# Attention and gated experts on one core: the order of the early expert tiles' transposes, gathers and activations

## The chip, the cores and the metric

One core of a Trainium2 chip runs the whole program. The metric is the device time of one execution in microseconds, from launch to end. Before the change the median of 3 runs is 470.3 us (469.93 to 471.26).

## What is computed

The inputs are q, k and v of shape (4, 8, 768, 64), a decay per head, a gate matrix of 8 experts with one more column for "local", and the experts' weights w1 (8, 512, 1024) and w2 (8, 1024, 512), all in fp32. First comes linear attention with decay, block by block along the sequence; its output is laid out as x with 3072 tokens of 512 numbers. Then each token goes through one expert:

```python
fresh_e = int(np.argmax(logits[b, s]))
e = fresh_e if s == 0 or local_gate[b, s] < 0.5 else prev_e
p = softmax(logits[b, s])
h = np.maximum(x[b, s] @ w1[e], 0.0)
out[b, s] = p[e] * (h @ w2[e])
```

The expert of a token can so depend on the token before it.

## The kernel before, in words

**Attention, 24 steps.** A step handles 128 tokens of one batch. TensorE makes scores, products with the state and the transposed output (lines 186 to 281); ScalarE copies the rows of x to `xn`, and a DMA writes them to `x_dram` (`rows_of`, line 269). `gates` and `logits` (lines 283 to 297) make the gate's logits of four steps at a time. Routing is computed on the side: `fresh_experts`, `along_sequences`, `experts_of`, `chances`, `ranks`, `masks` (lines 383 to 482), in three parts of the tokens, the third (i = 2) after the last step. `brought` and `by_slots` (lines 590 to 631) turn tokens into slots: `brought` is VectorE work, `by_slots` a sum on TensorE over all tokens that gives the token index of each slot (`gidx`), and its gate.

**The early tiles.** The routing of the first half of the tokens is known early, so five tiles of 128 tokens of one expert each (tiles 0 to 4) are computed while the second half is still being routed. A tile is: gather 128 rows of x (`ahead`, an indirect DMA issued by GpSimd, into `xgt[0]` or `xgt[1]` in turn); turn them so that the features lie on partitions (`xtt`); `hidden` for each half of the 1024 hidden numbers (64 TensorE instructions in all, then a Relu on ScalarE, line 738); `output` (16 TensorE instructions, line 742); `written` (gate on VectorE, line 768, and a scatter). Turning without TensorE takes two steps: `flipped` (line 716), one VectorE transpose of 32x32 blocks into `xqs[0]` (the tile `xlast`) or `xqs[1]` (the tile `lg`), and `moved` (line 720), 16 ScalarE copies of 32 partitions x 128 elements (line 725) that put the blocks in their places. `turned_in_blocks` is both. `turned` (line 710) does it with four TensorE transposes and a copy out of PSUM.

**The later tiles.** Tokens that remain go in pairs of tiles of one expert (`pair`, line 974), computed as a Winograd product of 7 instead of 8 block products: `sums_1`, `sums_2` and `sums_of_x` (lines 936 to 948) are VectorE sums of weight blocks and of x, `product_1` (line 953) and `product_2` (line 958) are TensorE. Within a pair numbered hooks take the steps of half tiles (`hooks_of_halves`, line 1123) and of others. With this data there are also three full tiles between pair 2 and pair 3 (`full`, line 1216).

**What sets the order.** Inside `manual_schedule` each named engine runs its instructions in the order in which the code writes them. For the attention and the early tiles these are TensorE, VectorE, SyncE and GpSimd, and ScalarE's order comes from a scheduler; from line 1175 on they are TensorE, VectorE, SyncE and ScalarE. Weights come over SyncE's queue (`weights`, line 670, skipped if the buffer already holds the expert; `weights_of`, line 677) into two buffers of w1 and w2 each, and a third that is shared by half and full tiles and, before that, by the 0/1 array that `brought` writes. From the early tiles to the first pair the code before reads, with the lines of the change in it:

```python
        turned_in_blocks(1)            # 902: tile 3, behind tokens_to_other_tiles
        hiddens(2); finished(2); weights(4)
        brought(1, (0, 1, 2, 3, 4))    # 906
        turned_in_blocks(0)            # 907: tile 4
        hiddens(3)                     # 908
        by_slots(1, (0, 1, 2, 3, 4))   # 910
        finished(3)                    # 912
...
        hidden(0, 0, 0)                # 1182: tile 4
        hidden(0, 0, 1)
        pair_turned(0); sums_1(0, range(4)); output(0, 0); pair_turned(1)
        sums_of_x(0)                   # 1188, then pair 0
```

Of the kernel before, what the change touches and what calls it, by code (L numbers as in the profile page):

```python
# [8 lines left out]
F32 = mybir.dt.float32  # L9
# [55 lines left out]
def kernel(  # L65
# [203 lines left out]
    def rows_of(s):  # L269
        px = pg.tile([P, DM], F32, name="pk1")  # L270
        for a in range(A):
            nc.tensor.transpose(px[:, P * a:P * a + P], xc[:, a, ORDER[s][0]], ident)
        if s + 1 < NS:
            xn = att.tile([P, DM], F32, name="xn", bufs=4)
        else:
            xn = xlast
        nc.scalar.copy(xn, px)


        queue = nc.scalar if s + 3 < NS else nc.sync  # L280
        queue.dma_start(out=x_dram[P * s:P * s + P, :], in_=xn)

    def gates(k):

        for d in range(DT):
            nc.tensor.matmul(pl[EP * d:EP * d + EP], lhsT=wgt[:, d], rhs=xc[:, d].rearrange("p b i -> p (b i)"),
                             start=True, stop=True, skip_group_check=True)
        lg = lgs[k] = rt.tile([P, B * P], F32, name="lg")
        nc.scalar.copy(lg, pl)
# [86 lines left out]
    def pool(i):  # L376
        return pools[i == 2]
# [5 lines left out]
    def fresh_experts(i):  # L383

        lo, hi = PARTS[i]
        n = hi - lo
        lg = lt[:, lo:hi, :E]
        if not i:
            nc.vector.memset(lt[0:1, :B, E:], -1.0)
        mx = nows["mx", i] = pool(i).tile([P, n], F32, name=f"mx{i}", bufs=1)  # L390
        nc.vector.tensor_reduce(mx, lg, axis=AX.X, op=ALU.max)
        top = pool(i).tile([P, n, E], F32, name=f"top{i}", bufs=1)
        nc.vector.tensor_tensor(top, lg, mx.unsqueeze(2).broadcast_to([P, n, E]), ALU.is_equal)
        nc.vector.tensor_tensor(top, top, down.unsqueeze(1).broadcast_to([P, n, E]), ALU.mult)
        best = pool(i).tile([P, n], F32, name=f"best{i}", bufs=1)
        nc.vector.tensor_reduce(best, top, axis=AX.X, op=ALU.max)
        mark = nows["mark"] = pool(i).tile([P, n], BF16, name=f"mark{i}", bufs=1)
        nc.vector.scalar_tensor_tensor(mark, lt[:, lo:hi, E], FRESH, best, ALU.is_le, ALU.mult)

    def along_sequences(i):  # L400
# [269 lines left out]
    def weights(g):  # L670

        experts[g] = e = expert(g)
        other = e != experts[g - 2]
        nc.sync.dma_start(out=w1t[g % 2], in_=w1_src(e), cond=other, cond_hint=False)
        nc.sync.dma_start(out=w2t[g % 2], in_=w2_src(e), cond=other, cond_hint=False)
# [8 lines left out]
    def w_of(p):  # L684
        return (p + 1) % 2
# [16 lines left out]
    def ahead(g, i):  # L702
        collect(xgt[i], *at(g))
# [3 lines left out]
            nc.tensor.transpose(pr[:, P * d:P * d + P], xgt[0][:, P * d:P * d + P], ident)  # L707
        nc.vector.tensor_copy(xtt[0].rearrange("p d i -> p (d i)"), pr)

    def turned(i, xt=None, copy=nc.vector.tensor_copy, xg=None):  # L710
        pt = pg.tile([P, DT, P], F32, name="po1")
        for d in range(DT):
            nc.tensor.transpose(pt[:, d], (xgt[i] if xg is None else xg)[:, P * d:P * d + P], ident)
        copy(xtt[i] if xt is None else xt, pt)

    def flipped(xq, xg):

        nc.vector.transpose(xq, xg)  # L718

    def moved(xt, xq, ks=range(4)):  # L720

        blocks = xq.rearrange("p (d j i) -> p d j i", j=4, i=QP)
        for k in ks:
            for j in range(4):
                nc.scalar.copy(xt[QP * j:QP * j + QP, :, QP * k:QP * k + QP], blocks[QP * k:QP * k + QP, :, j])  # L725

    def turned_in_blocks(i, xg=None):
        flipped(xqs[i], xgt[i] if xg is None else xg)
        moved(xtt[i], xqs[i])

    def hidden(i, w, half):
        ph = pg.tile([P, FT // 2, P], F32, name=f"ps{half}")
        for j in range(FT // 2):
            f = FT // 2 * half + j
            for d in range(DT):
                nc.tensor.matmul(ph[:, j], lhsT=w1t[w][:, d, P * f:P * f + P], rhs=xtt[i][:, d],  # L736
                                 start=(d == 0), stop=(d == DT - 1))
        nc.scalar.activation(hq[half, i], ph, ACT.Relu)  # L738

    def output(i, w):  # L740
        for f in range(FT):
            nc.tensor.matmul(pys[i], lhsT=hq[f // 4, i][:, f % 4], rhs=w2t[w][:, f], start=(f == 0), stop=(f == FT - 1))  # L742

    def apart(rows):
# [45 lines left out]
    with tc.manual_schedule(engines={PE, DVE, SP, POOL}):  # L790
# [16 lines left out]
        for s in range(NS):  # L807
            if s + LOADS - 1 < NS:
                loaded(s + LOADS - 1)
            if s + 3 < NS and s != 1:  # L810
                prepare(s + 3)
            if s in QUARTERS:
                j = QUARTERS.index(s)
                nc.sync.dma_start(out=w1t[0][:, j], in_=w1_src(0)[:, j])
            if s == NS - 4:
                nc.sync.dma_start(out=w2t[0], in_=w2_src(0))
                weights(0)
            if s == NS - 1:
                nc.sync.dma_start(out=w1t[1], in_=w1_src(1))
                nc.sync.dma_start(out=w2t[1], in_=w2_src(1))  # L820
                weights(1)
            if s + 1 < NS and s not in (1, 2, 3, 4, 5):
                scores(s + 1)
            from_state(s)
            if s % B == 1 and s > B:
                logits(s // B - 1)
            if s == 5:
                scores(6)
            extra_work(s, 0)
            if s % B == 0 and s:  # L830
                gates(s // B - 1)
            mix(s)
            if s == 0:
                update(0)
                query_powers(0)
            if s in (1, 2, 3, 4):
                scores(s + 1)
            if s == 1:
                query_powers(1)
                prepare(4)  # L840
                rows_of(0)
            if s:
                update(s)
            if s + 1 == NS:
                first_turned()
            if s > 1:
                rows_of(s - 1)
            extra_work(s, 1)
# [19 lines left out]
        def finished(g):  # L868
            output(g % 2, g % 2)
            written(g, g % 2)  # L870
# [3 lines left out]
            hidden(g % 2, g % 2, 1)  # L874


        hidden(0, 0, 0)
        rows_of(NS - 1)
        gates(NC - 1)
        ahead(2, 0)  # L880
        hidden(0, 0, 1)
        by_slots(0, (2, 3, 4))
        logits(NC - 1)
        xqs.extend((xlast, rt.tile([P, DM], F32, name="lg")))
        turned_in_blocks(1)
        fresh_experts(2)
        finished(0)
        weights(2)
        along_sequences(2)
        ahead(3, 1)  # L890
        turned_in_blocks(0)
        hiddens(1)
        experts_of(2)
        chances(2)
        finished(1)
        weights(3)
        ranks(2)
        masks(2)
        other_tiles()
        tokens_to_other_tiles()  # L900
        ahead(4, 0)
        turned_in_blocks(1)
        hiddens(2)
        finished(2)
        weights(4)
        brought(1, (0, 1, 2, 3, 4))
        turned_in_blocks(0)
        hiddens(3)
        weights_of(KA, w_of(0), (1,))
        by_slots(1, (0, 1, 2, 3, 4))  # L910
        weights_of(G2, 2)
        finished(3)


    def a1(p, i, k):
# [45 lines left out]
    def pair_ahead(p):  # L961
        for i in range(2):
            ahead(KA + 2 * p + i, i)

    def pair_turned(i):
        turned(i, xp(0, i), nc.scalar.copy)

    def pair_flipped(i):
        flipped(xqs[i], xgt[i])
# [4 lines left out]
    def pair(p, hooks={}, next=True, load=True, cond=None, write=True, further=True):  # L974
# [63 lines left out]
        gated(c01, a, g1)  # L1038
        hook(7)
        if next:  # L1040
            pair_moved(p + 1, 1)
        product_2(b, hs[:, 1], s2[:, 1], True)
        tt(hs[:, 3], h01, hs[:, 1], sub)
        stt(c10, b, g0, rest, ALU.mult, ALU.add)  # L1044
        hook(8)
        if next:
            sums_1(p + 1, (0, 1))
        product_2(c, hs[:, 2], b2(p, 0, 1), True)
        hook(9)
        product_2(b, hs[:, 0], s2[:, 0])  # L1050
        stt(c11, b, g0, rest, ALU.mult, ALU.add)  # L1051
        stt(c11, c, g0, c11, ALU.mult, ALU.add)
        hook(10)
        if next:
            sums_1(p + 1, (2, 3))
        product_2(a, h01, b2(p, 1, 0))
        gated(c00, a, g1)
# [117 lines left out]
    with tc.manual_schedule(engines={PE, DVE, SP, ACTE}):  # L1175
# [3 lines left out]
        pair_ahead(0)  # L1179
        rows_out(1)  # L1180
        ahead_half(0)
        hidden(0, 0, 0)
        hidden(0, 0, 1)
        pair_turned(0)
        sums_1(0, range(4))
        output(0, 0)
        pair_turned(1)
        sums_of_x(0)
        pair_ahead(1)
        written(4, 0)  # L1190
# [12 lines left out]
        def others():  # L1203
# [12 lines left out]
            def full(f, n=E):  # L1216

                i, w = f % 2, w_of_full(f)
                if f + 3 < n:
                    full_ahead(f + 3)  # L1220
                if not f:
                    weights_of(G1 + 1, w_of_full(1), cond=fulls > 1)
                if f + 1 < n:
                    turned_in_blocks(1 - i, rows[(f + 1) % 3])
                hidden(i, w, 0)
                hidden(i, w, 1)
                output(i, w)
                written(G1 + f, i)
                if f + 2 < n:
                    weights_of(G1 + f + 2, w, cond=fulls > f + 2)  # L1230
# [92 lines left out]
```

## Time and profile before

| | us |
|---|---|
| median of 3 runs | 470.3 (469.93 to 471.26) |
| the profiled execution, its own time | 468.88 |
| its span, first to last instruction | 467.2 |
| TensorE busy in it | 440.9 (94%) |
| VectorE, ScalarE, GpSimd busy | 271.8, 198.3, 112.2 |
| mean granted TensorE clock | 0.979 |

Stages of the span, by TensorE's first instruction in each: attention from 0, tile 0's hidden layer at 100.06, tile 1 at 118.42, tile 2 at 133.68, tile 3 at 155.46, tile 4 at 173.99, pair 0 at 188.96, the three full tiles at 287.31, pairs 3 to 7 from 336.14, and TensorE's last instruction at about 459.9. In a timeline row the columns are start, duration, engine, line, operation, output and input, partitions x elements, count, and in brackets the idle time just before and what ended it. "Granted clock" is the share of TensorE's full clock that the hardware allowed in a stretch.

### The profile page before, as it was taken

To read this page: it belongs to the slowest core of one execution; us is meant where nothing else is said; L and a number is where in the kernel's file an instruction comes from. 1 tells how busy PE (TensorE), PEld (TensorE's weight loads), DVE (VectorE), ACT (ScalarE), POOL (GpSimd) and SP (SyncE) were. 2 spreads that over 40 slices of the span, in tenths; PEclk is the share of its full clock that TensorE was granted. 3 is DMA by queue.
4 is the path that set the end of the run, shared out by engine and by line. 5 is a ranking of instruction groups with operands and counts; after the bars stand their busy time and mean duration, and the time that the engine had idled before them with its cause. 6 is when DMAs were issued, how large, how long until landed. Compare 5 with 4: busy or idle time off the path is not lost. (4 is left out here: it accounts for less than half of the span.)

```text
span 467.2 us, 10480 instructions
## 1 busy us (share of the span) xinstructions
PE 440.9 (94%) x4194; PEld 363.7 (78%) x4194; DVE 271.8 (58%) x544; ACT 198.3 (42%) x580; POOL 112.2 (24%) x120
## 2 busy tenths in 40 slices
PE   8999999999896699998999999799999999999993
PEld 7787787776773667877785999476698989899993
DVE  5456767831469515675463696010188787878661
ACT  3455666335501701551525347440055555656020
POOL 4476574400130021302320400110010202030101
PEclk9999999999999699999999999799999999999998
DMA  7999999967999379799994499958333848470101
GB/s 272 410 419 413 341 304 343 397 232 287 345 362 344 143 285 371 283 391 404 395 395 189 134 401 374 328 183 307 116 106 145 270 171 270 181 255 19 53 3 49
DMA packets 42576, 124.85 MB, mean 267 GB/s; under 512 B 3148, under 2 KB 3148, under 8 KB 40592
## 3 DMA queue, kind: packets, MB, share of 16 engines
q1 hardware_dynamic: 34976, 104.62, 60.6%
q0 software_dynamic: 4368, 13.90, 8.4%
q10 hardware_dynamic: 3168, 5.51, 3.1%
q8 instruction: 37, 0.61, 0.5%
q14 instruction: 27, 0.22, 0.1%
HBM read 124.02 MB, written 12.91 MB: 293 GB/s over the span
## 5 line engine op out<-in xcount | busy, mean ns | idle before, releaser
L736 PE MATMUL ps<-xt,w 128*128 128x128 f32 x512 | 61.5, 283 | 7.9 <-ACT xt L725 7.5
L736 PEld LDWEIGHTS ps<-xt,w 128*128 128x128 f32 x512 | 60.4, 198 | 10.9 <-ACT xt L725 8.4
L742 PE MATMUL pk<-w,h 128*128 128x512 f32 x128 | 59.6, 620 | 3.9 <-ACT h L738 3.9
L742 PEld LDWEIGHTS pk<-w,h 128*128 128x128 f32 x128 | 24.7, 199 | 33.1 <-issue 28.5
L698 POOL DMA_INDIRECT xg<-x_dram,gidx x25 | 27.9, 1117 | 64.5 <-DVE lg L718 23.3
L751 POOL DMA_INDIRECT out_dram<-y,sidx x14 | 14.7, 1051 | 115.4 <-DVE y L768 44.0
L212 DVE TENSOR_TENSOR sm<-ps,mask 128x512 f32<-128x512 f32 x46 | 29.6, 685 | 16.0 <-PE ps L208 8.5
L768 DVE TENSOR_SCALAR y<-pk,gate 128x512 f32<-128x512 f32 x8 | 5.9, 742 | 51.6 <-PE pk L742 30.2
L725 ACT COPY xp<-xlast 32x128 f32<-32x128 f32 x112 | 33.2, 296 | 2.6 <-DVE xlast L718 1.2
L725 ACT COPY xp<-lg 32x128 f32<-32x128 f32 x112 | 33.1, 296 | 2.6
L953 PEld LDWEIGHTS ps<-xp,w 128*128 128x128 f32 x256 | 30.3, 192 | 1.5 <-issue 1.3
L953 PE MATMUL ps<-xs,s 128*128 128x128 f32 x256 | 31.3, 275 | 0.1
L953 PE MATMUL ps<-xp,w 128*128 128x128 f32 x256 | 31.4, 276 | 0.0
L177 POOL TENSOR_TENSOR qd<-inp,lamq 128x512 f32<-128x512 f32 x20 | 25.6, 1279 | 21.4 <-PE po L235 9.5
L958 PE MATMUL pk<-w,h 128*128 128x256 f32 x128 | 30.5, 381 | 0.0
L958 PE MATMUL pk<-s,hsum 128*128 128x256 f32 x128 | 30.3, 380 | 0.0
L953 PEld LDWEIGHTS ps<-xs,s 128*128 128x128 f32 x256 | 29.9, 192 | 0.3 <-DVE xs L934 0.3
L248 PE MATMUL po<-sm,inp 128*64 128x128 f32 x384 | 27.9, 280 | 0.7 <-issue 0.6
L738 ACT ACTIVATE h<-ps 128x512 f32<-128x512 f32 x16 | 9.2, 597 | 43.4 <-PE ps L736 43.3
L248 PEld LDWEIGHTS po<-sm,inp 128*64 128x64 f32 x384 | 21.1, 136 | 7.9 <-issue 6.6
L725 ACT COPY xt<-xlast 32x128 f32<-32x128 f32 x64 | 18.9, 296 | 19.0 <-DVE xlast L718 17.6
L958 PEld LDWEIGHTS pk<-s,hsum 128*128 128x128 f32 x128 | 23.9, 190 | 3.3 <-DVE s L1044 0.2
(273 smaller groups left out, 794.7 us busy)
## 6 DMA issues: line engine op xcount, KB each, us to landing
w<-in_w_dram SPq DMA_DIRECT2D x43, 2048.0 KB, 11.8
inp<-in_qkv_dram SPq DMA_DIRECT2D x15, 1024.0 KB, 10.9
x_dram<-xn ACTq DMA_DIRECT2D x21, 256.0 KB, 7.4
inp<-in_qkv_dram SPq DMA_DIRECT2D x10, 512.0 KB, 6.7
inp<-in_qkv_dram SPq DMA_DIRECT2D x4, 768.0 KB, 6.7
w<-in_w_dram SPq DMA_DIRECT2D x4, 512.0 KB, 9.4
x_dram<-xn SPq DMA_DIRECT2D x2, 256.0 KB, 2.8
xg<-x_dram,gidx POOLq DMA_INDIRECT x25, 6.7
```

The costliest lines, as they stand in the source:

```text
L177: nc.gpsimd.tensor_tensor(qd, x[:, 0].rearrange("p (a i) -> p a i", i=P), lamq, ALU.mult)
L212: nc.vector.tensor_tensor(sm[:, u], ps[u], mask[:, u], ALU.mult)
L248: nc.tensor.matmul(head(a, u), lhsT=vn[:, a, u], rhs=sm[:, u, a], start=(not c and a < 2), stop=True, skip_group_check=True)
L698: nc.gpsimd.indirect_dma_start(out=xg, out_offset=None, in_=x_dram[:n, :], in_offset=bass.IndirectOffsetOnAxis(ap=gidx[i][:, j:j + 1], axi ...
L725: nc.scalar.copy(xt[QP * j:QP * j + QP, :, QP * k:QP * k + QP], blocks[QP * k:QP * k + QP, :, j])
L736: nc.tensor.matmul(ph[:, j], lhsT=w1t[w][:, d, P * f:P * f + P], rhs=xtt[i][:, d], start=(d == 0), stop=(d == DT - 1))
L738: nc.scalar.activation(hq[half, i], ph, ACT.Relu)
L742: nc.tensor.matmul(pys[i], lhsT=hq[f // 4, i][:, f % 4], rhs=w2t[w][:, f], start=(f == 0), stop=(f == FT - 1))
L751: apart(nc.gpsimd.indirect_dma_start(out=out, out_offset=bass.IndirectOffsetOnAxis(ap=sidx[i][:, j:j + 1], axis=0), in_=y, in_offset=None, ...
L768: nc.vector.tensor_scalar(yt[:, i], pys[i], gate_of(g), None, ALU.mult)
L953: nc.tensor.matmul(to[:, m], lhsT=a[:, k, P * m:P * m + P], rhs=b[:, k], start=(new and not m and not k), stop=(k == 1), skip_group_check= ...
L958: nc.tensor.matmul(to, lhsT=a[:, f], rhs=b[:, f], start=(new and not f), stop=(f == FT // 2 - 1), skip_group_check=True)
```

## The change

The turning of the early tiles is taken out of the stream just before each tile. Tile 1 is flipped, through the still unused hidden buffer `hq[1, 0]`, before tile 0's hidden layer; tiles 2, 3 and 4 are flipped one to two tiles before use, and each gather follows at once the flip that frees its buffer. The copies (`moved`) of tiles 3 and 4 are written behind the Relus of the tile before. The write of the last rows and `weights(1)` change places on SyncE's queue. `fresh_experts(2)` keeps its intermediates in an older buffer (`each0`), not in the new pool over the attention's memory. The sum of `by_slots(1, ...)` now stands between the two halves of tile 3's output instead of before the output. The first pair is turned with flips and copies too: both flips behind `sums_1`, the copies of its first tile on ScalarE between the two Relus of tile 4, those of its second tile on VectorE. In `pair` the 16 copies of the next pair's second tile are spread over four places; in `full` the copies follow the Relus.

```diff
-        mx = nows["mx", i] = pool(i).tile([P, n], F32, name=f"mx{i}", bufs=1)
+        if i == 2:
+            room = rt.tile([P, 2, NA, E], F32, name="each0", bufs=1).rearrange("p k n e -> p (k n e)")
+            mx, best, mark = (room[:, n * (E + k):n * (E + k) + n] for k in range(3))
...
-    def moved(xt, xq, ks=range(4)):
+    def moved(xt, xq, ks=range(4), copy=nc.scalar.copy):
...
-    def output(i, w):
-        for f in range(FT):
+    def output(i, w, fs=range(FT)):
+        for f in fs:
...
-                weights(1)
...
+        xqs.extend((xlast, rt.tile([P, DM], F32, name="lg")))
+        ahead(2, 0)
+        xq = hq[1, 0].rearrange("p f i -> p (f i)")
+        flipped(xq, xgt[1])
+        ahead(3, 1)
+        moved(xtt[1], xq, (0, 1))
         hidden(0, 0, 0)
         rows_of(NS - 1)
+        weights(1)
         gates(NC - 1)
-        ahead(2, 0)
+        moved(xtt[1], xq, (2, 3))
         hidden(0, 0, 1)
         by_slots(0, (2, 3, 4))
         logits(NC - 1)
-        xqs.extend((xlast, rt.tile([P, DM], F32, name="lg")))
-        turned_in_blocks(1)
         fresh_experts(2)
+        flipped(xqs[1], xgt[0])
+        ahead(4, 0)
+        moved(xtt[0], xqs[1])
         finished(0)
         weights(2)
         along_sequences(2)
-        ahead(3, 1)
-        turned_in_blocks(0)
+        flipped(xqs[0], xgt[1])
         hiddens(1)
+        moved(xtt[1], xqs[0])
         experts_of(2)
         chances(2)
+        flipped(xqs[1], xgt[0])
         finished(1)
         weights(3)
         ranks(2)
         masks(2)
         other_tiles()
         tokens_to_other_tiles()
-        ahead(4, 0)
-        turned_in_blocks(1)
         hiddens(2)
-        finished(2)
+        moved(xtt[0], xqs[1])
+        output(0, 0)
         weights(4)
         brought(1, (0, 1, 2, 3, 4))
-        turned_in_blocks(0)
+        written(2, 0)
         hiddens(3)
         weights_of(KA, w_of(0), (1,))
+        output(1, 1, range(FT // 2))
         by_slots(1, (0, 1, 2, 3, 4))
         weights_of(G2, 2)
-        finished(3)
+        output(1, 1, range(FT // 2, FT))
+        written(3, 1)
...
         hook(7)
         if next:
-            pair_moved(p + 1, 1)
+            moved(xp(p + 1, 1), xqs[1], (0,))
...
         ahead_half(0)
+        sums_1(0, range(4))
+        pair_flipped(0)
+        pair_flipped(1)
         hidden(0, 0, 0)
+        pair_moved(0, 0)
         hidden(0, 0, 1)
-        pair_turned(0)
-        sums_1(0, range(4))
+        moved(xp(0, 1), xqs[1], copy=nc.vector.tensor_copy)
         output(0, 0)
-        pair_turned(1)
         sums_of_x(0)
...
-                    turned_in_blocks(1 - i, rows[(f + 1) % 3])
+                    flipped(xqs[1 - i], rows[(f + 1) % 3])
                 hidden(i, w, 0)
                 hidden(i, w, 1)
+                if f + 1 < n:
+                    moved(xtt[1 - i], xqs[1 - i])
                 output(i, w)
```

The pieces (1,), (2,) and (3,) of the copies in `pair` follow in the same way behind hooks 8, 9 and 10.

More of the change, by code (lines that the diff above doesn't have):

```diff
@@ L389, in fresh_experts @@
             nc.vector.memset(lt[0:1, :B, E:], -1.0)
-        mx = nows["mx", i] = pool(i).tile([P, n], F32, name=f"mx{i}", bufs=1)
+        if i == 2:
+            room = rt.tile([P, 2, NA, E], F32, name="each0", bufs=1).rearrange("p k n e -> p (k n e)")
+            mx, best, mark = (room[:, n * (E + k):n * (E + k) + n] for k in range(3))
+            top, mark = room[:, :n * E].rearrange("p (n e) -> p n e", e=E), mark.bitcast(BF16)[:, :n]
+        else:
+            mx, best = (rt.tile([P, n], F32, name=f"{k}{i}", bufs=1) for k in ("mx", "best"))
+            top = rt.tile([P, n, E], F32, name=f"top{i}", bufs=1)
+            mark = rt.tile([P, n], BF16, name=f"mark{i}", bufs=1)
+        nows["mx", i], nows["mark"] = mx, mark
         nc.vector.tensor_reduce(mx, lg, axis=AX.X, op=ALU.max)
-        top = pool(i).tile([P, n, E], F32, name=f"top{i}", bufs=1)
         nc.vector.tensor_tensor(top, lg, mx.unsqueeze(2).broadcast_to([P, n, E]), ALU.is_equal)
         nc.vector.tensor_tensor(top, top, down.unsqueeze(1).broadcast_to([P, n, E]), ALU.mult)
-        best = pool(i).tile([P, n], F32, name=f"best{i}", bufs=1)
         nc.vector.tensor_reduce(best, top, axis=AX.X, op=ALU.max)
-        mark = nows["mark"] = pool(i).tile([P, n], BF16, name=f"mark{i}", bufs=1)
         nc.vector.scalar_tensor_tensor(mark, lt[:, lo:hi, E], FRESH, best, ALU.is_le, ALU.mult)
@@ L708, in first_turned @@
         nc.vector.tensor_copy(xtt[0].rearrange("p d i -> p (d i)"), pr)
[L710 to L714, printed above, removed]
     def flipped(xq, xg):
         nc.vector.transpose(xq, xg)
-    def moved(xt, xq, ks=range(4)):
+    def moved(xt, xq, ks=range(4), copy=nc.scalar.copy):
         blocks = xq.rearrange("p (d j i) -> p d j i", j=4, i=QP)
@@ L724, in moved @@
             for j in range(4):
[L725 to L729, printed above, removed]
+                copy(xt[QP * j:QP * j + QP, :, QP * k:QP * k + QP], blocks[QP * k:QP * k + QP, :, j])
     def hidden(i, w, half):
@@ L963, in pair_ahead @@
             ahead(KA + 2 * p + i, i)
-    def pair_turned(i):
-        turned(i, xp(0, i), nc.scalar.copy)
     def pair_flipped(i):
@@ L1046, in pair @@
         if next:
+            moved(xp(p + 1, 1), xqs[1], (1,))
             sums_1(p + 1, (0, 1))
@@ L1049, in pair @@
         hook(9)
+        if next:
+            moved(xp(p + 1, 1), xqs[1], (2,))
         product_2(b, hs[:, 0], s2[:, 0])
@@ L1054, in pair @@
         if next:
+            moved(xp(p + 1, 1), xqs[1], (3,))
             sums_1(p + 1, (2, 3))
```

## The prediction

> **What bounds the kernel now.** I read the page first, then TensorE's waits, then the timelines of TensorE, ScalarE and VectorE round the two longest waits. From the page, the shares and two rows of the 40 slices:
>
> ```profile
> PE 440.9 (94%) x4194; PEld 363.7 (78%) x4194; DVE 271.8 (58%) x544; ACT 198.3 (42%) x580; POOL 112.2 (24%) x120
> PE   8999999999896699998999999799999999999993
> PEclk9999999999999699999999999799999999999998
> ```
>
> TensorE is busy 94% of 467.2 us; two dips (slices 13 and 14, slice 26) each come with a lower granted clock. So time is won only where TensorE idles, runs at the low clock, or does work that another engine can do. TensorE's waits:
>
> ```profile
> PE ps L736 <- ACT xt L725: 7.5, 1, 7.5
> PE pk L742 <- ACT h L738: 3.9, 3, 3.1
> PE po L1101 <- ACT hs L1094: 1.6, 1, 1.6
> PE pr L406 <- DVE mark L398: 1.4, 1, 1.4
> ```
>
> All four lie where the diff works: tile 3's hidden layer waits for its copies, outputs wait for Relus, the half tile in pair 0 waits for its Relu, and routing waits for `mark`. TensorE's timeline gives the price of each, the slow running behind it included:
>
> ```profile
> 118.17 0.33 PE L406 MATMUL pr<-identb,mark 128*4 128x128 bf16 x3 [1.41 <-DVE mark L398]
> 118.42 7.41 PE L736 MATMUL ps<-xt,w 128*128 128x128 f32 x64
> 126.62 7.13 PE L742 MATMUL pk<-w,h 128*128 128x512 f32 x16 [0.63 <-ACT h L738]
> 133.68 7.38 PE L736 MATMUL ps<-xt,w 128*128 128x128 f32 x64
> 140.89 7.03 PE L742 MATMUL pk<-w,h 128*128 128x512 f32 x16
> 155.46 9.74 PE L736 MATMUL ps<-xt,w 128*128 128x128 f32 x64 [7.53 <-ACT xt L725]
> 297.71 10.11 PE L742 MATMUL pk<-w,h 128*128 128x512 f32 x16 [3.10 <-ACT h L738]
> ```
>
> The reader should see 9.74 and 10.11 us after the two long gaps where the same groups take 7.4 and 7.0 elsewhere. From VectorE's timeline, why the first gap is there, and how long the first pair's sums take:
>
> ```profile
> 149.52 0.69 DVE L718 STREAM_TRANSPOSE lg<-xg 128x512 f32<-128x512 f32 x1
> ...
> 177.40 1.22 DVE L931 TENSOR_TENSOR s<-w 128x1024 f32<-128x1024 f32 x1
> 178.65 1.22 DVE L931 TENSOR_TENSOR w<-w 128x1024 f32<-128x1024 f32 x1
> 179.79 1.22 DVE L932 TENSOR_TENSOR s<-s,w 128x1024 f32<-128x1024 f32 x1
> 181.05 1.22 DVE L932 TENSOR_TENSOR s<-w,s 128x1024 f32<-128x1024 f32 x1
> ```
>
> The flip of tile 3 stood behind all the routing sums (to 149.5), though its tokens had been known since before 100. On ScalarE, the copies and what they hold up:
>
> ```profile
> 120.85 5.10 ACT L725 COPY xt<-xlast 32x128 f32<-32x128 f32 x16 [3.94 <-DVE xlast L718]
> 125.97 1.08 ACT L738 ACTIVATE h<-ps 128x512 f32<-128x512 f32 x2
> ```
>
> **Early tiles: what goes.** (1) `mark`: VectorE's L391 waited 5.81 us for a store of x's rows, which SyncE issued only at 114.5, behind `weights(1)`. The store now precedes that, and the intermediates lie in an old buffer: -1.41 us. (2) Tile 1's Relus stood behind 16 copies; tile 1 goes from its hidden layer to its output in 126.62 - 118.42 = 8.20, tile 2 in 140.89 - 133.68 = 7.21: -0.99. (3) Tile 3's gap: -7.53. (4) Its slow clock: L736 at 155.46 to the slots' sum at 165.04 is 9.58, against 7.21: -2.37. Sum -12.3.
>
> What is late next? Tile 3's copies now end by about 130, because its flip precedes tile 1's hidden layer. The Exp of `chances` (0.28 us) queues behind them: to 130.2, then 2.6 us of VectorE as before, tile 4's flip 0.7 and tile 1's gate; the routing chain starts near 134.1, before 134.46. It then takes the same 15.1 to 149.2, `brought` 6.2 more, to 155.4. TensorE reaches the slots' sum, half an output into tile 3, at 131.4 + 4 x 7.1 - 3.5 = 156.3. So the cover is 0.9 us: every us that `brought` is later than that is paid. With the sum ahead of the whole output, as before, TensorE would reach it at 152.8 and wait 2.6. Weights: 2 MB land 8.0 to 20.9 us after issue, 12.2 in the median, the longest those queued behind two others; tile 2's are issued near 114.5 and 117 for use at 131 and 139, later ones at the same distance from TensorE: no cost. The gathers are issued earlier and land in 6.5 to 7.7, far ahead. On GpSimd they stand before tile 0's scatter, 1.0 each, beside TensorE. So TensorE ends tile 3 at 161.7 instead of 173.97.
>
> **First pair: what comes in.** Two groups of four TensorE transposes go: tile 4 to pair 0 takes 188.96 - 173.97 = 14.99 now, and 7.2 + 7.0 = 14.2 without them, -0.8. But the order now is: VectorE does `sums_1`, then both flips; ScalarE does the Relu of tile 4's first half, then the 16 copies that wait for the first flip, then the second half's Relu. That Relu was free of such waits; behind it in ScalarE's queue nothing is urgent, but half an output on TensorE needs it. With tile 4's start as 0: `sums_1` starts at 177.40 - 173.97 = 3.43 (after the gate, `both_halves` and `rows_out`), ends at 8.3, the flip at 8.9; 16 copies end at 14.0; the Relu lets TensorE go at 14.7 (in the trace 0.65 after the Relus' start). TensorE has done the hidden layer and half the output at 7.2 + 3.5 = 10.7. A new gap of 4.0 us. The w1 of the pair is issued when tile 3's hidden layer ends, near 152.8, when one load is ahead of it, and so lands between 160.8 and 165.0, just before `sums_1` wants it at 165.2; the gathers, issued near 159.6 and 160.9, land near 166 and 167.5, before the flip at 170.
>
> What does a gap of 4.0 cost in clock? The row: after the gap of 3.10 the clock read 0.50 from 297 to 303 and the output took 3.0 us longer; after 7.53 it was 2.4; gaps of 1.4 and 1.6 left 1.00. The Trainium skill ("TensorE: Matmul & The Clock Gate", Part 1) says that the array falls to half clock after at least one idle window of about 3.4 us, a free-running one, and comes back after a busy one. By the rule the 3.10 gap would cost only itself; the row says that a mostly idle window is enough. I go by the row: the full tiles' gain below is 6.6, not 3.6, and the new gap costs 2.6 more (bounds 0, if the clock should hold as after 1.6, and 3.4, an estimate from the row: the low clock lasted 6.8 us, half of it lost). Then half an output, 3.5: pair 0 starts at 14.7 + 3.5 + 2.6 = 20.8 instead of 14.99: **+5.8**.
>
> The second tile's 16 copies on VectorE have no row of that shape. Nearest: 0.17 (128x15) and 0.29 (128x128 out of PSUM), so 2.7 to 4.6 us beside ScalarE's 5.1: hidden, but `sums_of_x` waits for both; done at 16.0, wanted at 22.6. If copies took twice that it would still hold.
>
> **Pairs.** Spreading the second tile's copies lets the half tile's Relu pass after 4 copies (1.3 us) instead of 16: -1.62. `sums_of_x` wants them at 219.9, they ended at 211.3 and now end near 213.5: covered. Without half tiles in the hooks ScalarE's order stays.
>
> **Full tiles.** The Relus pass before the copies. First tile 287.31 to 297.71: 10.40, against 7.14 for the third: -3.26; its output 9.95 against 6.97: -2.98; the second tile's 7.50: -0.36. Sum -6.6. The copies then lie beside the 7.0 us of output (5.1 us): covered. The next weights are issued by TensorE's own progress and land 8 to 13 us later for use 21 us later.
>
> **The sum.** -12.3 + 5.8 - 1.6 - 6.6 = -14.7. The profiled execution, 468.88 (span 467.2), would become 454.2; it lies 1.4 under the median of 470.3, which so becomes **455.6**. About 0.3% is what a measurement can tell from no change.
>
> **Rivals.** *No new gap in the first pair* (0.17): if the second half's Relu were not held up, the section is 14.2, so -0.8 in place of +5.8: 449.0. For it speaks only that my times rest on one execution. Against: both queues are in program order, and `sums_1` cannot start before the gate of tile 3. *The early part stays bound by VectorE or the gathers* (0.14): the routing chain 3 us later than reckoned puts `brought` 2 us beyond its cover, and with a slow clock behind it costs 2 to 5; or the pair's gathers land 3 to 5 us later beside three weight loads, and each us is a us of gap. 458 to 461. Against: gathers beside loads took 6.3 to 7.7. *Slower than before* (0.03): the split copies make every pair late. They stand at four places in ScalarE's queue, each behind what the hooks put there; if the last piece slipped by more than the 6.4 us to `sums_of_x` in pairs that have `next` (7), TensorE would wait at the second product, 3 us and a slow clock each; from 2.1 us in each of the 7 the 14.7 are eaten, and at 4.5 the time is 455.6 + 31.5 = 487. Against: in pairs 3 to 7 nothing else stands between the pieces. *The change does nothing in the early part* would need tile 3's flip still behind the routing; its place in VectorE's order excludes it.
>
> **Numbers.** The likeliest case has 0.66, with 452.5 to 457.0 of its own (clock cost 0 to 3.4, cover of `brought`). 449.0 has 0.17, 458 to 461 has 0.14, slower 0.03. The range 448.5 to 460 leaves out 0.1 to 0.2: half of the late cases, the slower one, and tails. Faster 0.96, same 0.01, slower 0.03.
>
> **What would show it.** Tile 3's L736 without a gap and at clock 1.00; tile 3's end near 161.7; a gap of about 4 us in the middle of tile 4's output, released by ScalarE's Relu right behind 16 copies, with a granted clock of 0.5 after it; no wait of L1101; three full tiles in 42 us. Wrong: if the Relu of tile 4 is not late, if a wait for `brought` stands at the slots' sum, or if weights are what the new gap waits for.

## The result and the profile after

The change takes the kernel from 470.12 us (median of 4, 468.14 to 471.26) to 453.32 us (median of 4, 452.58 to 454.92): ratio 0.9652, 95% interval 0.9609 to 0.9694. Forecast was 455.6. The profiled execution has a span of 451.0 us (before 467.2).

The page after, the same three rows as before:

```profile
PE 434.5 (96%) x4186; PEld 360.3 (80%) x4186; DVE 277.4 (61%) x562; ACT 201.5 (45%) x594; POOL 109.3 (24%) x120
PE   8999999899999996999999999999999999999993
PEclk9999999999999998999999999999999999999998
```

The two dips of before (slices 13 and 14, slice 26) are gone; a new one stands in slice 16. TensorE's waits name it; the three other waits that the change went for are no longer in the list:

```profile
PE pk L737 <- ACT h L733: 3.6, 1, 3.6
PE pk L789 <- POOL ident masks.py:199: 2.0, 1, 2.0
```

(The second was there before, at the kernel's start.) TensorE's timeline from tile 3 to pair 0:

```profile
146.81 7.31 PE L731 MATMUL ps<-xt,w 128*128 128x128 f32 x64
...
157.39 2.17 PE L619 MATMUL pr<-w,lane 128*128 128x190 bf16 x24
...
162.91 7.39 PE L731 MATMUL ps<-xt,w 128*128 128x128 f32 x64
170.14 3.60 PE L737 MATMUL pk<-w,h 128*128 128x512 f32 x8
177.30 5.40 PE L737 MATMUL pk<-w,h 128*128 128x512 f32 x8 [3.56 <-ACT h L733]
182.53 1.95 PE L957 MATMUL ps<-xp,w 128*128 128x128 f32 x16
```

Tile 3 (146.81) starts without a wait and at full clock. Tile 4's output is torn: half of it in 3.60, 3.56 us of idling, the other half in 5.40. ScalarE's timeline says why:

```profile
166.82 0.60 ACT L733 ACTIVATE h<-ps 128x512 f32<-128x512 f32 x1 [12.01 <-PE ps L731]
171.72 4.90 ACT L724 COPY xp<-xlast 32x128 f32<-32x128 f32 x16 [4.30 <-DVE xlast L717]
176.65 0.60 ACT L733 ACTIVATE h<-ps 128x512 f32<-128x512 f32 x1
```

The second Relu runs right behind the 16 copies, and these behind the flip, which VectorE made at 170.98, after `sums_1`. The full tiles, in TensorE's timeline, now follow each other in 14.0 us each:

```profile
278.24 7.31 PE L731 MATMUL ps<-xt,w 128*128 128x128 f32 x64
285.38 7.03 PE L737 MATMUL pk<-w,h 128*128 128x512 f32 x16
292.25 7.31 PE L731 MATMUL ps<-xt,w 128*128 128x128 f32 x64
```

By stages of TensorE's timeline, each from the start of one group to the start of the next, in the profiled executions:

| stretch, us | before | after | difference | forecast |
|---|---|---|---|---|
| start to tile 0 | 100.06 | 101.30 | +1.24 | 0 |
| tile 0 to tile 4 | 73.93 | 61.61 | -12.32 | -12.3 |
| tile 4 to pair 0 | 14.97 | 19.62 | +4.65 | +5.8 |
| first seven products of pair 0 | 13.33 | 12.65 | -0.68 | 0 |
| rest of pairs 0 to 2 | 85.02 | 83.06 | -1.96 | -1.6 |
| three full tiles | 48.83 | 42.04 | -6.79 | -6.6 |
| pairs 3 to 7 and the end | 131.06 | 130.72 | -0.34 | 0 |

The profiled executions of the 14 kernels here start tile 0 between 100.1 and 105.5 us, though all run the same attention before it, so a microsecond in the medians settles little. The stretches behind tile 0 repeat to 0.1 us in most of these kernels where nothing differs (the last one, to the end, to 0.3 us). Two are less steady: behind a gap that lowers the clock a stretch varies by over 1 us, and the stretch from tile 0 to tile 4 with the old order took 73.93 us in the kernel before and 72.21 us in full_alone, which has the same code there. I judge by the stretches, and give the medians beside them. The forecast of 455.6 lies 2.3 above the measured median, and the range held. Behind tile 0 the gain is 17.4 us against 14.7 forecast.

### The profile page after: what moved, and what is told of

Its sections match the earlier page's. It is cut to its first block, busy times and chain, and to the rows that moved or that the text cites. A ratio compares the mean times of both kernels' runs of the same rounds, so it can differ in the third digit from the quotient of the medians.

```text
span 451.0 us, 10496 instructions
## 1 busy us (share of the span) xinstructions
PE 434.5 (96%) x4186; PEld 360.3 (80%) x4186; DVE 277.4 (61%) x562; ACT 201.5 (45%) x594; POOL 109.3 (24%) x120
## 4 chain that ended last, share of the span: by engine, by line
PE 80%; DMA 7%; issue 6%; DVE 4%; ACT 1%; POOLq 0%; POOL 0%; DVEq 0%
PE ps L957 12%; PE pk L737 12%; PE ps L731 11%; PE pk L962 11%; DMA out_dram<-y,sidxp 6%; PE po L248 5%; PE po L957 5%; PE pl L962 4%; PE ps L208 3%; PE pk L272 3%; PE pk L262 2%; PE pr L1118 2%; PE po L235 2%; PE pr L1096 2%; PE pl L286 1%
## 5 line engine op out<-in xcount | busy, mean ns | idle before, releaser
L737 PE MATMUL pk<-w,h 128*128 128x512 f32 x128 | 58.5, 609 | 3.6 <-ACT h L733 3.6
L731 PEld LDWEIGHTS ps<-xt,w 128*128 128x128 f32 x512 | 58.2, 192 | 3.0 <-issue 2.3
L731 PE MATMUL ps<-xt,w 128*128 128x128 f32 x512 | 59.1, 276 | 0.3 <-DVE xt L713 0.3
L737 PEld LDWEIGHTS pk<-w,h 128*128 128x128 f32 x128 | 24.2, 195 | 31.3 <-issue 26.2
L724 ACT COPY xp<-xlast 32x128 f32<-32x128 f32 x128 | 37.8, 295 | 6.0 <-DVE xlast L717 4.3
L703 POOL DMA_INDIRECT xg<-x_dram,gidx x25 | 25.8, 1031 | 58.0 <-DVE lg L717 25.4
L957 PEld LDWEIGHTS ps<-xp,w 128*128 128x128 f32 x256 | 30.5, 192 | 1.6 <-issue 1.3
L957 PE MATMUL ps<-xp,w 128*128 128x128 f32 x256 | 31.3, 276 | 0.0
L957 PE MATMUL ps<-xs,s 128*128 128x128 f32 x256 | 31.2, 275 | 0.0
L957 PEld LDWEIGHTS ps<-xs,s 128*128 128x128 f32 x256 | 29.9, 192 | 0.0
L962 PEld LDWEIGHTS pk<-w,h 128*128 128x128 f32 x128 | 23.6, 191 | 3.3 <-issue 0.6
```

The source lines that it names most:

```text
L703: nc.gpsimd.indirect_dma_start(out=xg, out_offset=None, in_=x_dram[:n, :], in_offset=bass.IndirectOffsetOnAxis(ap=gidx[i][:, j:j + 1], axi ...
L957: nc.tensor.matmul(to[:, m], lhsT=a[:, k, P * m:P * m + P], rhs=b[:, k], start=(new and not m and not k), stop=(k == 1), skip_group_check= ...
L962: nc.tensor.matmul(to, lhsT=a[:, f], rhs=b[:, f], start=(new and not f), stop=(f == FT // 2 - 1), skip_group_check=True)
```

## Experiments

All but full_alone are the changed kernel with one thing altered, or two where the text says so. "Behind tile 0" is the profiled span from tile 0's first product on: 367.1 before, 349.7 after. The ratios are to runs of the kernel before that were taken together with each experiment.

**relu_first**: both Relus of tile 4 ahead of the copies.

```diff
         hidden(0, 0, 0)
-        pair_moved(0, 0)
         hidden(0, 0, 1)
+        pair_moved(0, 0)
```

> The change with one step moved: the first pair's 16 ScalarE copies stand behind both Relus of tile 4. Theory A, the new gap of 3.56 us in tile 4's output (and 1.8 us of slow clock behind it) is nothing but ScalarE's program order, the Relu behind copies that wait for the flip behind sums_1: the gap goes, the stretch from tile 4's start to pair 0 falls from 19.6 to 14.2 us, the time by 5.4 to about 448. Theory B, the pair's inputs are late anyway (gathers, w1, copies), so the gap only moves to pair 0's first products: TensorE waits 1 us or more at L957, and the time falls by less than 4.

Measured: 452.88 us (ratio to before 0.9673, 0.9638 to 0.9708), the same as the change within the interval. But the stretch did fall from 19.62 to 14.10, as theory A says; the gap in tile 4 is gone. Pair 0's first seven products grew from 12.65 to 16.49 instead. TensorE's timeline of this run, then VectorE's:

```profile
190.79 2.76 PE L957 MATMUL po<-xs,w 128*128 128x128 f32 x16 [2.09 <-DVE part L1004]
```

```profile
186.33 1.22 DVE L937 TENSOR_TENSOR s<-w 128x1024 f32<-128x1024 f32 x1 [2.12 <-DMA w<-in_w_dram]
187.59 1.22 DVE L937 TENSOR_TENSOR w<-w 128x1024 f32<-128x1024 f32 x1
188.73 0.70 DVE L717 STREAM_TRANSPOSE lg<-xg 128x512 f32<-128x512 f32 x1
189.36 0.65 DVE L1003 TENSOR_TENSOR part<-part,ps 128x512 f32<-128x512 f32 x1
190.04 0.69 DVE L1004 TENSOR_TENSOR part<-part,po 128x512 f32<-128x512 f32 x1
```

`sums_2` waits 2.12 us for the pair's second weights; the part sums stand behind it on VectorE, and TensorE needs the PSUM bank that L1004 reads. So theory A is right about the cause of the gap. The two signs of theory B came as well, a wait of over 1 us at L957 and a gain below 4, but through an input that B had not named: the second weights. This wait of 2.09 with its slow clock, 3.8 us in all, eats most of the 5.5. Behind tile 0: 348.0.

**flips_first**: the two flips ahead of `sums_1`.

```diff
-        sums_1(0, range(4))
         pair_flipped(0)
         pair_flipped(1)
+        sums_1(0, range(4))
```

> The change with the two flips of the first pair ahead of sums_1 on VectorE; the copies still stand between the Relus. Theory A': what makes the copies late is sums_1 (4.8 us) in front of the flips, not the gathers: the first flip runs when its gather has landed, 160.7 + 6.5 = 167.2, the copies end at 172.9, the Relu at 173.5, TensorE wants it at 173.7: a gap under 0.5 us, time 5 us below the change, about 448. Theory B: the gathers beside three weight loads land only about when sums_1 is done (near 171): the gap stays at 3 us or more and the time within 1 us of the change.

Measured: 451.52 us (0.9651, 0.9623 to 0.9679). The first flip waited 1.69 us for its gather, the gap in tile 4's output shrank to 0.56, the stretch to 14.92: A' holds as to the cause, and B falls. Two of its sizes were missed: the gap was to be under 0.5, and the time was to fall by 5, against 2.5 behind tile 0. Again pair 0's seven products take longer (14.56): `sums_2` waits 1.53 for the same load, TensorE 1.51. Here the clock stayed at 1.00. Behind tile 0: 347.2.

**pair_on_pe**: the first pair turned by TensorE again, in the old order of that block (`pair_turned(0)`, `sums_1`, `output`, `pair_turned(1)`).

> The change with the first pair turned by TensorE again, as before the change; all else stays. If this part of the change is a loss by itself: tile 4's start to pair 0 is 15.0 us instead of 19.6, the granted clock stays 1.00 there, and the time falls by 4.6, to about 448.7. If the flips of the first pair had been a gain hidden under something else (later products starting smoother), the 0.7 us that pair 0's seven first products lost before the change come back, and the gain is 3.9.

Measured: 451.42 us (0.9668, 0.9639 to 0.9696). Tile 4 to pair 0 takes 14.97, as before the change; seven products 14.47, with a wait of 1.29 for L1013, the same part sum. Behind tile 0: 347.0. So in the change as it stands, turning the first pair off TensorE costs 2.7 us, less than the 4.6 or 3.9 expected: 4.65 are lost before the pair, and 1.8 come back, because the gap hides the late weights (`sums_2` waits 1.31 for them here, and not at all in the change).

**relu_first_w2_first**: two alterations, `relu_first`, and the half tile's loads behind the pair's second weights.

```diff
         by_slots(1, (0, 1, 2, 3, 4))
-        weights_of(G2, 2)
...
         weights_of(KA, w_of(0), (2,))
+        weights_of(G2, 2)
```

> relu_first with one more move: the half tile's two loads (weights_of(G2, 2)) stand on SyncE's queue behind the pair's second weights instead of ahead of them. Theory D: in relu_first the gap turned into a wait for these second weights: sums_2 of pair 0 waited 2.1 us on VectorE for the load that stands behind two 2 MB loads which are wanted 12 us later, the part sums behind sums_2 and with them TensorE (2.1 us and slow clock, stretch of pair 0's first seven products 16.5 us instead of 12.65). With the order turned the load lands about 8 us earlier: no wait in pair 0, tile 4 to pair 0 14.1, first seven products 12.6, the time 5.4 under the change (about 448). Rival E: VectorE itself is too full here (sums of x, gate, flips, sums_2): TensorE still waits 1 us or more for L1004.

Measured: 449.49 us (0.9625, 0.9579 to 0.9671). TensorE's timeline:

```profile
163.51 7.39 PE L731 MATMUL ps<-xt,w 128*128 128x128 f32 x64
170.74 7.03 PE L737 MATMUL pk<-w,h 128*128 128x512 f32 x16
177.60 1.95 PE L956 MATMUL ps<-xp,w 128*128 128x128 f32 x16
```

14.09 to pair 0, 12.65 for the seven products, no wait of over 0.3 us behind tile 0. Theory D holds, E falls. Behind tile 0: 344.3, so 5.4 under the change, as forecast. Against `w2_first`, measured together with it, the medians differ by 4.8. This is the lowest median and the shortest span behind tile 0 of all versions here.

**on_pe_w2_first**: `pair_on_pe` with the loads in that order.

> pair_on_pe (the first pair turned by TensorE) with the same reordered loads. Theory D: its seven first products fall from 14.5 to about 12.8; what is left against relu_first_w2_first is TensorE's 8 transposes and the short waits by them, 0.8 to 1.2 us. That is all that turning the first pair off TensorE can bring.

Measured: 450.51 us (0.9653, 0.9600 to 0.9705). 14.97 and 13.05; behind tile 0 345.7. Against relu_first_w2_first that is 0.88 + 0.40 = 1.3 us, slightly over the 0.8 to 1.2 expected: all that taking the first pair off TensorE brings here. The medians (1.0 apart) cannot tell this, the stretches can.

**w2_first**: the change with only the loads in that order.

> The change with only the loads reordered, the Relu still behind the copies. Theory D: in the change the gap of 3.56 us already gives the load its time, nothing waited for it, so nothing changes: tile 4 to pair 0 19 to 20.5 us (by the clock's phase), seven products 12.65, time within noise of the change. Rival: if the loads' order matters by itself, the stretch of pair 0 changes by over 0.5 us.

Measured: 454.30 us (0.9705, 0.9655 to 0.9756). Gap of 3.56 as in the change, 20.93 to pair 0 (19 to 20.5 expected; slow clock behind the gap, as explained below), seven products 12.64. As D says: the load was no bound while the gap hid it.

**copies_whole**: the 16 copies of the next pair's second tile in one piece.

> The change with the second tile's 16 copies in pairs in one piece again. Theory A, the pieces only let the half tile's Relu pass in pair 0: TensorE's wait of 1.6 us for L1099 comes back once, the stretch of pairs 0 to 2 grows from 95.7 to 97.4, the time by 1.7 (454.9 or so). Rival: the pieces also smooth other pairs, or cost there: pairs 3 to 7 would differ by more than 0.3 us from the change's.

Measured: 456.15 us (0.9747, 0.9707 to 0.9786). The wait is back, from TensorE's waits:

```profile
PE po L1102 <- ACT hs L1095: 1.6, 1, 1.6
```

Rest of pairs 0 to 2: 84.98 against 83.06, +1.9; pairs 3 to 7 130.74 against 130.72. With this data the pieces help once, and cost nothing elsewhere.

**slots_before_output**: `by_slots(1, ...)` ahead of the whole output of tile 3.

> The change with the slots' sum ahead of the whole output of tile 3, as before the change. VectorE ended brought at 156.2 in the change, TensorE gets to the sum at 154.0. If the half output ahead is a cover for brought: a wait of 2.3 us at L619 appears, by brought. If a gap of 2.3 us can lower the clock (3.1 and 3.6 did, 1.6 did not): 1.5 to 3 us more on what follows, +4 to +5 in all; if not: +2.3. The slots come about 1 us earlier, so that part of the gap in tile 4's output could shrink only if the gathers, and not sums_1, held it: expected unchanged at 3.6.

Measured: 457.24 us (0.9764, 0.9737 to 0.9790). TensorE's timeline, and the same stretch in windows (width, busy time of TensorE, its weight loads, VectorE, ScalarE and GpSimd, granted clock, DMA share, GB/s):

```profile
158.66 3.68 PE L619 MATMUL pr<-w,lane 128*128 128x190 bf16 x24 [2.28 <-DVE w L609]
```

```profile
155.00:158.70 3.70, 1.42 (x14) 1.25 (x13) 3.70 (x5) 0.60 (x1) 0.00 (x0) 0.97 0.75 237
158.70:162.20 3.50, 3.50 (x25) 3.35 (x24) 0.57 (x1) 0.00 (x0) 0.98 (x1) 0.54 1.02 410
```

A wait of 2.28 for `brought`, then a granted clock of 0.54 over the next 3.5 us. The change takes 2.0 from the sum to the output, this one 3.52; tile 0 to tile 4 grows by 3.96. The half output ahead is worth 4.0 us. The gap in tile 4's output stays (3.68).

**flip3_late**: tile 3's flip and copies behind the routing sums.

```diff
         along_sequences(2)
-        flipped(xqs[0], xgt[1])
         hiddens(1)
-        moved(xtt[1], xqs[0])
...
         tokens_to_other_tiles()
+        flipped(xqs[0], xgt[1])
+        moved(xtt[1], xqs[0])
         hiddens(2)
```

> The change with tile 3's flip and copies behind the routing sums again. Theory A, the place of this one flip in VectorE's order made the 7.5 us gap of before: a gap of 6 to 8 us ahead of tile 3's hidden layer comes back, with about 2.4 us of slow clock, tile 4 starts 8 to 10 us later, time about 462. Rival, the other moves (earlier gathers, Relus not behind copies, the slots' sum inside the output) had a share: the gap is below 4 us.

Measured: 464.49 us (0.9904, 0.9871 to 0.9937).

```profile
158.44 9.47 PE L731 MATMUL ps<-xt,w 128*128 128x128 f32 x64 [7.29 <-ACT xt L724]
```

The gap of before is back, with its slow clock; tile 0 to tile 4 grows by 9.6. The place of this one flip, with the copies that follow it, makes three quarters of the early gain.

**mark_in_new_pool**: the intermediates of `fresh_experts(2)` in the new pool, as before the change.

```diff
-        if i == 2:
-            room = rt.tile([P, 2, NA, E], F32, name="each0", bufs=1).rearrange("p k n e -> p (k n e)")
...
+        mx, best = (pool(i).tile([P, n], F32, name=f"{k}{i}", bufs=1) for k in ("mx", "best"))
+        top = pool(i).tile([P, n, E], F32, name=f"top{i}", bufs=1)
+        mark = pool(i).tile([P, n], BF16, name=f"mark{i}", bufs=1)
```

> The change with fresh_experts(2)'s intermediates in the new pool again, x's last rows still stored early. The new pool's memory is free when the last store of rows has landed: issued at 101.6, the landing is near 110, and VectorE reaches L394 at 111.6. If the store's place in SyncE's queue was what held it: no wait, time as the change (within 0.3 us in the stretch from tile 0 to tile 1). If the buffer was what counted: 1.4 us of wait at the mark's matmul, as before.

Measured: 454.16 us (0.9699, 0.9660 to 0.9738). VectorE's timeline:

```profile
116.74 0.25 DVE L394 TENSOR_REDUCE mx<-lt 128x12 f32<-128x96 f32 x1 [5.95 <-DMA x_dram<-xn]
```

The wait is back to its length, though the store was issued 13 us earlier: it took 15.3 us to land, behind two 2 MB weight loads issued just before it on the same queue. `mark` is ready only at 118.1 and TensorE idles 0.94 before its product, tile 0 to tile 4 is 1.0 longer. My expectation (landing near 110) fails: the buffer counts.

**store_late**: `weights(1)` ahead of the stores, intermediates in the old buffer.

> The change with weights(1) ahead of the last rows' stores on SyncE again, the intermediates still in the old buffer. The stores go out near 115 instead of 101.6 and 108. The first that uses the new pool is then tile 0's gated output at 118.1, when they have landed (2 to 3 us): if either half of the remedy is enough, no wait and the time of the change; else a wait of up to 1.4 us, and tile 3's flip into xlast (120.3 in the change) waits for the second store.

Measured: 453.28 us (0.9685, 0.9658 to 0.9713). No wait at the mark, tile 0 to tile 4 61.62, as the change. The stores went out at 115.28 and 115.73. So moving the store brought nothing here; the buffer alone does it.

**full_alone**: the kernel before, with only the full tiles' copies behind the Relus.

> The kernel before with only the full tiles' copies put behind the Relus. If the full tiles' gain stands alone: the three tiles take 42.0 instead of 48.8 us, no slow clock there, time 6.8 below before (ratio about 0.9855), the early part as before. Rival: the gain needs the rest of the change (loads of the full tiles earlier); then a wait for weights shows at L736 or L742 there and the stretch stays above 44.

Measured: 463.23 us (0.9906, 0.9872 to 0.9941). The three full tiles take 42.04, to the hundredth what they take in the change: the gain stands alone. The median falls by 4.1, not 6.8, and the profiled span behind tile 0 by 8.8, of which 1.7 is the early part: its code is that of before, but the mark cost 0.40 instead of 1.41, and the slow clock behind tile 3's gap less. The stretch is certain; the median carries the spread of the rest.

## Why the prediction held, point by point

*Early tiles, -12.3 against -12.32.* Tile by tile, from start to start, the change is -1.49 (tile 0, with the mark), -0.71 (tile 1, 0.99 forecast), -7.69 (tile 2, with tile 3's gap) and -2.43 (tile 3, with the slow clock). That the sum agrees to the hundredth is in part luck: the stretch before varies by 1.7 between executions. Three experiments bear on the terms: tile 3's flip (9.6), the half output ahead of the slots' sum (4.0, where the text had reckoned a bare 2.6 of waiting: the slow clock behind it was left out), the mark. `brought` ended at 156.3, TensorE came at 157.39: the cover, 0.9 forecast, was 1.1.

*The mark: right size for this execution, wrong cause.* The text said that the wait went because the store now precedes `weights(1)`, and named the buffer second. It is the buffer; the early store still lands behind the loads that were issued before it.

*The first pair, +5.8 against +4.65.* The mechanism and each of its times came as reckoned: `sums_1` at 3.29 after tile 4's start (forecast 3.43), end of the copies at 13.71 (14.0), TensorE going on at 14.39 (14.7). The gap was 3.56 instead of 4.0. The slow clock was sized at 2.6, and cost 1.8 in this execution; in the seven runs that have such a gap (3.56 to 3.68) the half output behind it took 5.40, 6.32, 6.33, 6.33, 6.45, 6.58 and 6.70 instead of 3.62, so 2.7 more in the median. The size was right, and the profiled execution a cheap one: the clock was low for 3.4 us there, and for 6.8 in the six others.

*The rival without the gap would have missed.* I gave 449.0 for it, as if nothing stood behind the gap. relu_first shows that 3.8 of those us come back from pair 0's sixth product on: with the gap closed the weights' load comes 2 us too late. The likeliest case did not need this, the rival's number did.

*Not in the sum*: -0.68 in pair 0's first products. on_pe_w2_first leaves 0.40 of it to the turning on TensorE (its last copy is late for `sums_of_x`); the rest is argued, not shown: `sums_2` waited 0.2 for the second weights before the change.

*Pairs and full tiles*: -1.96 and -6.79 against -1.6 and -6.6; copies_whole (1.9) and full_alone (6.79) confirm both by themselves. With -0.68, -0.34 at the end and a first pair that cost less than forecast, nearly every difference went the same way, so the gain was underrated by 2.7 behind tile 0.

## What to carry to other kernels

On engines that run in program order, ask of every moved block what stands behind it: here a block moved to help TensorE put a Relu that TensorE wanted at once behind 16 copies that nobody wanted yet. Price a gap with the slow clock behind it, and before claiming the gain from closing one, look up when the next input (here a weight load that stood behind two loads, the first of which TensorE used 14 us later) really lands. Where medians of whole runs scatter by microseconds, compare stretches between fixed points of the timeline.

## What the runs showed of the hardware

The clock falls after shorter gaps than the prediction had seen. Gaps of 1.29 to 1.63 us left it at 1.00 in these runs. One of 1.77 us (relu_first, attention, ending at 85.62), 2.09 and 2.28 us were each followed by 3.4 us at half clock, 3.10 us by 6.8 us, one and the same gap of 3.6 us by either 3.4 or 6.8 us, and 7.53 us by 10.2 us, part of which lies in the gap itself. The Trainium skill ("TensorE: Matmul & The Clock Gate", Part 1) asks for at least one idle window of about 3.4 us; the runs decide, and they say that 1.77 us of idling can do.

From relu_first's windows, columns as above:

```profile
189.00:190.80 1.80, 0.01 (x1) 0.01 (x1) 1.77 (x4) 0.00 (x0) 1.01 (x1) 1.00 1.03 423
190.80:192.40 1.60, 1.60 (x12) 1.60 (x13) 1.56 (x2) 1.11 (x2) 0.00 (x0) 0.86 1.01 415
192.40:195.80 3.40, 3.40 (x20) 3.40 (x19) 2.15 (x4) 0.63 (x1) 0.00 (x0) 0.57 0.99 361
```

The 0.86 of the second row puts the fall at 191.94, 1.15 us after TensorE has taken up work again; the clock is back at 195.36. This fits a judgement made at fixed times over the stretch of 3.41 us before, and the traces bear it out. Every low stretch measured lasted 3.41, 6.83 or 10.24 us, and two falls in one trace lie whole multiples of 3.41 apart: 86.13 and 191.94 (31 times) in relu_first, 158.48 and 182.37 (7 times) in slots_before_output, 155.95 and 190.09 (10 times) in flip3_late, 150.13 and 296.91 (43 times) before the change. In the 3.41 us before each of these falls, and before that of the change at 177.79, TensorE had idled at least 1.77 us. So where a gap lies against these times decides its price, which explains 1.8 us of loss in one execution and 2.7 in another for the same gap. That about half of such a stretch must be idle is an inference from these runs; no run placed a gap on purpose.

A 256 KB store issued behind two 2 MB loads on one queue took 13.9 us (the change) and 15.3 us to land, against 2.3 where the profile shows no traffic ahead of it (before, 114 to 115.2 us). VectorE's 16 copies of 32 partitions x 128 elements took 4.10 us (the change; 3.69 in flips_first), ScalarE's 4.90.
